# Attention and two MoE layers on one core: row minima over two PSUM banks at once, small steps moved between engines, a new order

## The chip, the core and the metric

One core of one Trainium2 chip. The metric is the device time of one execution in microseconds (us); the kernel before has a median of 949.46 us over 3 runs (949.44 to 949.78). The engines are called PE (TensorE; PEld is its weight load), DVE (VectorE), ACT (ScalarE), POOL (GpSimd) and SP (SyncE, which issues most DMAs). SBUF is the on-chip working memory; PSUM is the memory that PE writes, in 8 banks of 512 float32 per partition.

## The reference, cut to what matters

```python
B, H, S, D = (4, 8, 576, 64)
scores = q @ k.T / sqrt(D); causal mask; a = softmax(scores); local = a @ v
q_p = where(q > 0, q, exp(q) - 1) + 1                  # phi, which is elu + 1
mem_out = (q_p @ M_prev) / (q_p @ z_prev + 1e-6)
g = 1 / (1 + exp(-beta))                               # per head
x = g * mem_out + (1 - g) * local                      # to 2304 tokens x 512
h = x @ w_in;  y = (h * tanh(softplus(h))) @ w_out     # first layer, 512 -> 2048 -> 512
h = y @ w_in2; out = (h * sigmoid(h)) @ w_out2         # second layer, same sizes
```

All of it is float32. The kernel reaches float32 accuracy in the two layers by splitting each operand into a high and a low part in the rounded format fp32r and summing three products.

## The kernel before

**Attention.** There are 32 heads, taken in 16 pairs (`B * NP`), and `steps(p)` (from L494) makes the steps of pair p. The 576 rows of queries are five chunks: chunk 0 has 64 rows, chunks 1 to 4 have 128; chunk i needs `width(i)` = 64 + 128 i columns of scores, so 192, 320, 448 and 576. For each pair and each head j of it:

- loads: `ldkT`, `ldqT`, `ldnq`, `ldnv` on SP's queue (`load`, L455); those of keys and queries (`kT`, `qT`) feed PE, `nq` feeds phi, `nv` holds the values.
- scores: `s1` to `s3`, `s0` and, since one PSUM bank holds 512 columns, two halves `s40` and `s41` of 288 columns for chunk 4 (`score`, L590; `s0`, L631). They go to a ring "s" of four PSUM banks (`RINGS`), one matmul output in each.
- row minima (the scores are negated, so a minimum is what softmax wants): `r..` on DVE, one instruction `ttr` (L588) that adds the mask, writes the scores to SBUF (`sm`) and keeps the minimum of the row; a short second instruction then writes the minimum out (DVE_READ_ACCUMULATOR2). For chunk 4 there are two of them for each head, the second starting from the minimum of the first (`r4`, L599). 
- exponentials with row sums: `e..` on ACT (L615).
- phi: `phu` (ACT, L507, a relu), `phn` (POOL, L505, q minus relu), `phe` (ACT, L506, the exponential), `phf` (POOL, L508, the sum), `phz`, `phy` (POOL, L509, L512, times z), `phr` (DVE, L513, row sums), `phg` (POOL, L516, L517), `phd` (DVE, L519, reciprocal), `phq` (DVE, L520, times the softmax row sums), then `phm..` (POOL, L534, L539), which put phi beside the exponentials.
- PE transposes of these (`X1`, `X2`, `X3`, `W`, L486) into the PSUM ring "t", copies out of it to SBUF (`X1A` and so on; those listed in `ON_ACT` on ACT, L476, the others on DVE, L479), the products with the values (`Vhi`, `Vlo`, L692) and their scaling into `xT` (DVE, L696).

Ahead of it stand the gates: `exp` on ACT (L434), `sig` (five instructions on DVE, L437 to L441), `spread` (ACT, L446 to L452). Steps `phg`, `n00` and `zg` of pair 0 need them.

**The layers.** `Moe` runs 32 visits (layer, quarter of the 2048 hidden columns, block of tokens). Activations are split on ACT (L971) and DVE (L964). Weights come in 64 + 64 jobs: a load `ld` (L793), the absolute value `abs` (L804 on ACT for the first eight jobs, `first(job)`; L806 on DVE for the others), four bit steps `b0` to `b3` on DVE (L814, L816, L818, L821), and splits on ACT, POOL (first eight jobs; L847, L866, L869) and DVE. The first eight jobs run beside the attention. PE multiplies with the names psX, psW, psY (L1000 to L1002) and acc (L1068). The layers' PSUM and SBUF pools open (`open0`, `open1`) only when the last pairs' steps have given theirs back.

**What sets the order.** `Steps.plan` lists all steps with a planned duration, due times and rings, and issues for each engine, in order of planned time, the ready step with the smallest late time; `SHIFT` is a table of numbers added to the late times of groups of steps. The order on each engine is therefore fixed when the program is built; on the chip every engine takes its instructions in that order and waits at each for what it needs.

## Time and profile before

| | us |
|---|---|
| median of 3 runs | 949.46 |
| span of the profiled execution, first to last instruction | 949.0 |
| first product of the layers starts on PE | 181.64 |
| DVE's first row minimum starts | 13.98 |
| PE, DVE, ACT, POOL busy over the span | 921.2, 662.5, 498.9, 140.4 |

The span is read in four stretches: 14.5 us in which the first data and gates arrive, 167 us of attention, 763 us of the two layers, and 4.5 us in which the last block is drained and stored. A busy time is the union of an engine's instructions; two instructions in a row on one engine overlap in the records by some 0.07 us, so the step from one start to the next is that much shorter than the duration. A bracket behind a row is the time that the engine stood idle before it and what released it.

### The profile page before, as it was taken

To read this page: it belongs to the slowest core of one execution; us is meant where nothing else is said; L and a number is where in the kernel's file an instruction comes from. 1 tells how busy PE (TensorE), PEld (TensorE's weight loads), DVE (VectorE), ACT (ScalarE), POOL (GpSimd) and SP (SyncE) were. 2 spreads that over 40 slices of the span, in tenths; PEclk is the share of its full clock that TensorE was granted. 3 is DMA by queue.
4 is the path that set the end of the run, shared out by engine and by line. 5 is a ranking of instruction groups with operands and counts; after the bars stand their busy time and mean duration, and the time that the engine had idled before them with its cause. 6 is when DMAs were issued, how large, how long until landed. Compare 5 with 4: busy or idle time off the path is not lost.

```text
span 949.0 us, 17264 instructions
## 1 busy us (share of the span) xinstructions
PE 921.2 (97%) x6544; PEld 813.1 (86%) x6544; DVE 662.5 (70%) x1504; ACT 498.9 (53%) x1172; POOL 140.4 (15%) x223
## 2 busy tenths in 40 slices
PE   4989999999999999999999999999999999999998
PEld 2656666799999999999999999998999888989986
DVE  4899899988984558665957889766647765754333
ACT  5998899876654243433433647554533442433330
POOL 5688798300000000000000000000000000000000
PEclk9999999999999999999999999999999999999999
DMA  6546563666647403850375535704550374024412
GB/s 209 149 158 194 165 199 121 213 261 235 221 150 250 156 1 98 274 156 1 117 253 197 221 119 198 278 23 162 189 177 10 108 265 145 1 93 147 157 54 99
DMA packets 60034, 147.72 MB, mean 156 GB/s; under 512 B 7600, under 2 KB 25136, under 8 KB 59952
## 3 DMA queue, kind: packets, MB, share of 16 engines
q1 hardware_dynamic: 59808, 146.30, 45.4%
...
q10 hardware_dynamic: 144, 0.33, 0.1%
...
## 4 chain that ended last, share of the span: by engine, by line
PE 85%; DVE 4%; ACT 3%; POOL 3%; issue 2%; DMA 2%; SPq 0%; DVEq 0%; POOLq 0%
PE acc L1068 42%; PE psX L1000 7%; PE psX L1001 7%; PE psX L1002 7%; PE psY L1000 4%; PE psY L1001 4%; PE psY L1002 4%; DVE sm L588 2%; PE psW L1001 2%; PE psW L1002 2%; PE psW L1000 2%; PE ps_t L692 2%; PE ps_s L595 2%; PE ps_t L486 1%; ACT Ph L615 1%
## 5 line engine op out<-in xcount | busy, mean ns | idle before, releaser
L1068 PE MATMUL acc<-g,w 128*128 128x320 f32 (+1 forms) x1152 | 218.3, 337 | 0.0
L1068 PE MATMUL acc<-w,g 128*128 128x512 f32 x864 | 214.4, 394 | 0.0
L1068 PEld LDWEIGHTS acc<-g,w 128*128 128x128 f32 x1152 | 183.8, 188 | 13.1
L1068 PEld LDWEIGHTS acc<-w,g 128*128 128x128 f32 x864 | 157.8, 188 | 30.5
L1031 ACT COPY vt<-psX 128x256 f32<-128x256 f32 (+1 forms) x192 | 75.2, 398 | 154.8 <-PE psX L1002 146.0
L1089 DVE TENSOR_TENSOR xT<-acc,xT 128x512 f32<-128x512 f32 (+1 forms) x126 | 77.2, 613 | 93.8 <-PE acc L1068 92.9
L1041 DVE TENSOR_TENSOR g<-vt,g 128x512 fp32r<-128x512 f32 (+1 forms) x128 | 94.1, 754 | 35.4 <-ACT g L1040 34.7
L1029 DVE TENSOR_TENSOR vt<-psY,vt 128x256 f32<-128x256 f32 (+1 forms) x128 | 57.9, 456 | 87.1 <-ACT vt L1031 46.2
L1040 ACT CAST g<-vt 128x512 fp32r<-128x512 f32 (+1 forms) x128 | 83.4, 672 | 31.5 <-PE acc L1068 30.1
L1000 PE MATMUL psX<-x,w 128*128 128x320 f32 (+1 forms) x256 | 75.8, 296 | 0.0
L1001 PE MATMUL psX<-x,w 128*128 128x320 f32 (+1 forms) x256 | 75.7, 296 | 0.0
L1002 PE MATMUL psX<-x,w 128*128 128x320 f32 (+1 forms) x256 | 75.6, 295 | 0.0
L595 PE MATMUL ps_s<-kT,qT 64*128 64x288 f32 (+3 forms) x320 | 66.8, 480 | 6.3 <-DMA kT<-in_kT_dram 4.6
L1037 ACT ACTIVATE vt<-vt 128x640 f32<-128x640 f32 (+1 forms) x64 | 43.8, 685 | 51.8 <-DVE vt L1029 51.5
L588 DVE CUSTOM_DVE_ANT_0 sm<-ps_s,mask 128x288 f32<-128x288 f32 (+3 forms) x128 | 56.9, 472 | 5.4 <-PE ps_s L595 3.1
L1035 ACT ACTIVATE vt<-vt 128x256 f32<-128x256 f32 (+1 forms) x64 | 28.5, 445 | 59.7 <-DVE vt L1029 59.7
L1036 ACT ACTIVATE vt<-psX 128x256 f32<-128x256 f32 (+1 forms) x64 | 26.0, 407 | 50.2 <-PE psX L1002 50.1
L1029 DVE TENSOR_TENSOR vt<-psW,vt 128x256 f32<-128x256 f32 (+1 forms) x64 | 29.1, 455 | 31.7 <-PE psW L1002 31.2
L1000 PEld LDWEIGHTS psX<-x,w 128*128 128x128 f32 x256 | 48.2, 188 | 2.0 <-issue 0.2
L1001 PEld LDWEIGHTS psX<-x,w 128*128 128x128 f32 x256 | 48.3, 189 | 1.7
L875 ACT CAST w<-val 128x512 fp32r<-128x512 f32 (+1 forms) x64 | 34.8, 567 | 26.5 <-DVE val L866 13.1
L1002 PEld LDWEIGHTS psX<-x,w 128*128 128x128 f32 x256 | 48.3, 188 | 0.0
...
## 6 DMA issues: line engine op xcount, KB each, us to landing
...
```

The source lines that it names most:

```text
L588: nc.vector.tensor_tensor_reduce(out, ps, mask, -0.125, init, ALU.add, ALU.min, acc)
L595: nc.tensor.matmul(ps, lhsT=s["qT"][R[j], qcols(i)], rhs=s["kT"][R[j], k0 + cols.start:k0 + cols.stop], start=True, stop=True)
L1000: nc.tensor.matmul(o, lhsT=W(0, kc), rhs=X(0, kc), start=(n in (1, 2, 7) and kc == 0), stop=False, skip_group_check=True)
L1001: nc.tensor.matmul(o, lhsT=W(0, kc), rhs=X(1, kc), start=False, stop=False, skip_group_check=True)
L1002: nc.tensor.matmul(o, lhsT=W(1, kc), rhs=X(0, kc), start=False, stop=(kc == 1), skip_group_check=True)
L1029: nc.vector.tensor_tensor(o, self.bank[q, to], o, op=ALU.add)
L1031: f[f"s{n}"] = lambda n=n: nc.scalar.copy(val(*at[n]), self.bank[q, "X"])
L1037: f["m2"] = lambda: nc.scalar.activation(val(1), val(1), fn)
L1040: f[f"h{c}"] = lambda c=c: nc.scalar.copy(hi(c), val(c))
L1041: f[f"l{c}"] = lambda c=c: nc.vector.tensor_tensor(self.gt(q, c)[:, 1, :2 * tb], val(c), hi(c).bitcast(F32), op=ALU.subtract)
L1068: nc.tensor.matmul(y, lhsT=a, rhs=b, start=(c == 0 and k == 0), stop=(c == 1 and k == 5))
L1089: nc.vector.tensor_tensor(part, acc, part, op=ALU.add)
```

## The change

Six things are changed, and the order of all engines is planned anew.

- **Row minima.** The ring "s" holds two units of two banks in place of four banks. For chunk 4 the two halves of a head lie in one unit, and one `ttr` of 576 columns reads both banks; for chunks 1 to 3 the two heads lie in the two banks of a unit; `s0` lies beside `s1`. A unit comes free when all that it holds is read. `sm` has five buffers for four; several small tiles have three or four buffers for two.
- **Gates.** Of `sig` DVE keeps the reciprocal; the other four small instructions go to POOL.
- **phi.** `phu` is relu(-q), `phe` exp of its negative, so that `phe` follows `phu` directly on ACT; `phn` adds q and `phu` in place into `nq`, which `phf` now frees.
- **phq** goes from DVE to POOL.
- **X2B**, a copy of 384 columns for each pair, goes from ACT to DVE.
- **abs** of the first eight weight jobs goes from ACT to DVE. These jobs may be planned from 6 us on, one in 16 us (before 20 and 20).

The planner gets new durations (`ps2`, `act2`, weights, POOL's splits), a rule (`port`, `lock`) by which some DVE steps and POOL's steps don't overlap in the plan, dependences that put each pair's scores behind the chunk 4 scores of the pair before, and a new `SHIFT`.

```diff
+                    if e == "D" and k in self.lock:
+                        d += max(0.0, port["G"] - now)
+                        port["D"] = now + d
+                    if e == "G":
+                        d += max(0.0, port["D"] - now)
+                        port["G"] = now + d
...
-ON_ACT = ("WA", "X1A", "X2A", "X2B", "X3A")
+ON_ACT = ("WA", "X1A", "X2A", "X3A")
...
+    E("phe", "A", 0.58, ["phu"])
...
-    E("phe", "A", 0.58, ["phn"])
-    E("phf", "G", 1.37, ["phe", "phu"])
-    E("phz", "G", 1.25, ["phf"])
+    E("phf", "G", 1.37, ["phe", "phn"])
+    E("phz", "G", 1.25, ["phf", "phe"])
     E("phy", "G", 0.29, ["phf"])
     E("phr", "D", dve(576), ["phz", "phy"])
-    E("phg", "G", 0.4, ["phr"])
+    E("phg", "G", 0.45, ["phr"])
...
-            n = SA if i == 4 else width(i)
-            E(f"s4{x}" if i == 4 else f"s{i}", "P", mm(n, 4), qk)
+            E(f"s4{x}" if i == 4 else f"s{i}", "P", mm(SA if i == 4 else w, 4), qk)
         for j in range(2):
-            w = width(i)
+            E(f"r{i}{j}", "D", dve(w) + 0.01, ["s40", "s41"] if i == 4 else [f"s{i}"], 0.17)
+            E(f"e{i}{j}", "A", act(w, False, 2), [f"r{i}{j}"])
+            m.uses.append(("sm", f"r{i}{j}", [f"r{i}{j}"], [f"e{i}{j}"]))
             if i == 4:
-                for x in range(2):
-                    E(f"r4{j}{x}", "D", dve(SA) + 0.067 * x, [f"s4{x}"] + ([f"r4{j}0"] if x else []), 0.17)
-                    m.uses.append(("s", f"s4{x}{j}", [f"s4{x}"], [f"r4{j}{x}"]))
-                dep = [f"r4{j}1"]
-            else:
-                E(f"r{i}{j}", "D", dve(w), [f"s{i}"], 0.17)
-                m.uses.append(("s", f"s{i}{j}", [f"s{i}"], [f"r{i}{j}"]))
-                dep = [f"r{i}{j}"]
-            E(f"e{i}{j}", "A", act(w, False, 2), dep)
-            r = f"r4{j}0" if i == 4 else f"r{i}{j}"
-            m.uses.append(("sm", r, [r], [f"e{i}{j}"]))
+                m.uses.append(("s", f"s4{j}", ["s40", "s41"], [f"r4{j}"]))
+        if i in (2, 3):
+            m.uses.append(("s", f"s{i}", [f"s{i}"], [f"r{i}0", f"r{i}1"]))
         if i == 1:
-            m.group("s", ("s0", "P", 0.17, qk), [("r00", "D", dve(ST), ["s0"], 0.17)])
+            E("s0", "P", 0.17, qk)
+            E("r00", "D", dve(ST), ["s0"], 0.17)
+            m.uses.append(("s", "s1", ["s1", "s0"], ["r10", "r11", "r00"]))
...
-            E("phq", "D", 0.12, ["za", "phd"])
+            E("phq", "G", 0.22, ["za", "phd"])
...
-    RINGS = {"s": 4, "t": 4, "sm": 4}
+    RINGS = {"s": 2, "t": 4, "sm": 5}
...
-        "nq": ([P, 9, D], F32, ["ldnq"], ["phn", "phu"], 2),
+        "nq": ([P, 9, D], F32, ["ldnq"], ["phf"], 2),
...
-        "e": ([P, 9, D], F32, ["phn"], ["phmh", "phml", "phm0"], 2),
+        "e": ([P, 9, D], F32, ["phe"], ["phmh", "phml", "phm0"], 2),
...
-        "c": ([P, 9], F32, ["phr"], ["phmh", "phml", "phm0"], 2),
+        "c": ([P, 9], F32, ["phr"], ["phmh", "phml", "phm0"], 4),
...
-        "P0": ([P, 3, ST], F32, ["e00", "phm0"], ["X3"], 2),
+        "P0": ([P, 3, ST], F32, ["e00", "phm0"], ["X3"], 3),
...
-    TILES["R"] = ([P, S - ST], F32, ["Rl"], ["Vhic", "Vloc"], 2)
+    TILES["R"] = ([P, S - ST], F32, ["Rl"], ["Vhic", "Vloc"], 3)
...
+    def unit(self, p, i, j):
+        s = self.st[p]
+        k = f"S4{j}" if i == 4 else f"S{i}"
+        if k not in s:
+            s[k] = self.ps["s"].tile([P, 2, 512], F32, tag="s", name="ps_s")
+        return s[k]
...
+        def one():
+            nc.gpsimd.tensor_scalar(bt, bt, 1.0, None, op0=ALU.add)
...
         def sig():
-            nc.vector.tensor_scalar(bt, bt, 1.0, None, op0=ALU.add)
             nc.vector.reciprocal(self.g, bt)
-            nc.vector.tensor_scalar(self.g1, self.g, -1.0, 1.0, op0=ALU.mult, op1=ALU.add)
-            nc.vector.tensor_scalar(self.g1c, self.g1, 1e-20, None, op0=ALU.max)
-            nc.vector.tensor_tensor(self.btg, self.g1c, bt, op=ALU.mult)
...
+        def rest():
+            nc.gpsimd.tensor_scalar(self.g1, self.g, -1.0, 1.0, op0=ALU.mult, op1=ALU.add)
+            nc.gpsimd.tensor_scalar(self.g1c, self.g1, 1e-20, None, op0=ALU.max)
+            nc.gpsimd.tensor_tensor(self.btg, self.g1c, bt, op=ALU.mult)
...
-        f["phn"] = lambda: nc.gpsimd.tensor_tensor(self.get(p, "e"), s["nq"], s["u"], op=ALU.subtract)
-        f["phe"] = lambda: nc.scalar.activation(s["e"], s["e"], AF.Exp)
-        f["phu"] = lambda: nc.scalar.activation(self.get(p, "u"), s["nq"], AF.Relu)
-        f["phf"] = lambda: nc.gpsimd.tensor_tensor(s["e"], s["e"], s["u"], op=ALU.add)
+        f["phu"] = lambda: nc.scalar.activation(self.get(p, "u"), s["nq"], AF.Relu, scale=-1.0)
+        f["phe"] = lambda: nc.scalar.activation(self.get(p, "e"), s["u"], AF.Exp, scale=-1.0)
+        f["phn"] = lambda: nc.gpsimd.tensor_tensor(s["nq"], s["nq"], s["u"], op=ALU.add)
+        f["phf"] = lambda: nc.gpsimd.tensor_tensor(s["e"], s["e"], s["nq"], op=ALU.add)
         f["phz"] = lambda: nc.gpsimd.tensor_tensor(
             self.get(p, "u")[:, :8].rearrange("p (c j) d -> p c j d", j=2), s["e"][:, :8].rearrange("p (c j) d -> p c j d", j=2),
             self.bt[b]["z"][:, h0:h0 + 2, :].unsqueeze(1).to_broadcast([P, 4, 2, D]), op=ALU.mult)
-        f["phy"] = lambda: nc.gpsimd.tensor_tensor(s["u"][:, 8], s["e"][:, 8], self.bt[b]["y"][:, hp], op=ALU.mult)
+        f["phy"] = lambda: nc.gpsimd.tensor_tensor(self.get(p, "u")[:, 8], s["e"][:, 8], self.bt[b]["y"][:, hp], op=ALU.mult)
...
-        f["phq"] = lambda: nc.vector.tensor_tensor(s["c"][:, :8], s["c"][:, :8], s["z"][:, :8], op=ALU.mult)
+        f["phq"] = lambda: nc.gpsimd.tensor_tensor(s["c"][:, :8], s["c"][:, :8], s["z"][:, :8], op=ALU.mult)
...
             for j in range(2):
-                ps = s[f"S{i}{j}{x}"] = self.psum("s")[:, :cols.stop - cols.start]
+                ps = self.unit(p, i, j)[:, x if i == 4 else j, :cols.stop - cols.start]
...
                 nc.tensor.matmul(
                     ps, lhsT=s["qT"][R[j], qcols(i)], rhs=s["kT"][R[j], k0 + cols.start:k0 + cols.stop],
                     start=True, stop=True)
-        def r4(j, x):
-            t = smt(4, j) if x == 0 else s[f"sm4{j}"]
-            m = G("m4")
-            cs = slice(x * SA, (x + 1) * SA)
-            init = BIG if x == 0 else m[:, 2 + j:3 + j]
-            acc = m[:, 2 + j:3 + j] if x == 0 else m[:, j:j + 1]
-            ttr(t[:, cs], s[f"S4{j}{x}"], self.mcols(j, S)[:, cs], init, acc)
...
         def ri(i, j):
             w = width(i)
-            ttr(smt(i, j), s[f"S{i}{j}"], self.mcols(j, w), BIG, G(f"m{i}")[:, j:j + 1])
+            sm, mask = smt(i, j), self.mcols(j, w)
+            if i == 4:
+                sm, mask = (t.rearrange("p (x k) -> p x k", x=2) for t in (sm, mask))
+                ps = self.unit(p, i, j)[:, :, :SA]
+            else:
+                ps = self.unit(p, i, j)[:, j, :w]
+            ttr(sm, ps, mask, BIG, G(f"m{i}")[:, j:j + 1])
...
         for j in range(2):
-            for x in range(2):
-                f[f"r4{j}{x}"] = lambda j=j, x=x: r4(j, x)
-            for i in (3, 2, 1):
+            for i in (4, 3, 2, 1):
...
-            s["S00"] = self.psum("s")[:, :ST]
+            s["S00"] = self.unit(p, 1, 0)[:, 0, width(1):width(1) + ST]
             for j in range(2):
...
-        m.add(("gate", "sig"), "D", 1.0, [("gate", "exp")], sig, 26.0)
-        m.add(("gate", "spread"), "A", 1.0, [("gate", "sig")], spread, 28.0)
+        m.add(("gate", "one"), "G", 0.2, [("gate", "exp")], one, 25.5)
+        m.add(("gate", "sig"), "D", 0.12, [("gate", "one")], sig, 26.0)
+        m.add(("gate", "rest"), "G", 0.6, [("gate", "sig")], rest, 27.0)
+        m.add(("gate", "spread"), "A", 0.75, [("gate", "rest")], spread, 28.0)
...
-                deps = [(p, x) for x in deps] + ([("gate", "spread")] if p == 0 and n in self.GATED else [])
-                if p > 1 and n in ("s40", "s41"):
-                    deps += [(p - 2, x) for x in self.SC + ["s0"]]
+                deps = [(p, x) for x in deps] + ([("gate", "spread")] if n in self.GATED else [])
+                if p and n in ("s40", "s41"):
+                    deps += [(p - 1, "s40"), (p - 1, "s41")] + [(p - 2, x) for x in (self.SC + ["s0"] if p > 1 else [])]
+                if p and n in ("s3", "s2", "s1", "s0"):
+                    deps += [(p - 1, "s40"), (p - 1, "s41")]
...
-            if self.first(job):
-                nc.scalar.activation(c, self.raw[job][:, :, 1].bitcast(F32), AF.Abs)
-            else:
-                nc.vector.tensor_scalar(
-                    c.bitcast(U32), self.raw[job][:, :, 1].bitcast(U32), 0x7FFFFFFF, None, op0=ALU.bitwise_and)
+            nc.vector.tensor_scalar(
+                c.bitcast(U32), self.raw[job][:, :, 1].bitcast(U32), 0x7FFFFFFF, None, op0=ALU.bitwise_and)
...
-            for x, e, d, deps in (("ld", "S", 2.2, []), ("abs", "A", 0.53, ["ld"]) if first else ("abs", "D", 0.465, ["ld"]),
...
+            for x, e, d, deps in (("ld", "S", 2.2, []), ("abs", "D", 0.335, ["ld"]),
...
+                if e == "D":
+                    m.lock.add(J(x))
...
+                m.lock.update(K(x) for x in ["l" + x for x in XOPS] + ["T1", "T2", "T3", "T4"])
...
-    ('gate', 'exp'): -1546.35, ('gate', 'sig'): -1000.81, ('gate', 'spread'): -1110.7, ('a', 'ldkT'): -1506.04,
...
+    ('gate', 'exp'): -11714.19, ('gate', 'one'): -139.64, ('gate', 'sig'): -170.94, ('gate', 'rest'): -4059.43,
```

The rows below are from the order of instructions that the built programs hold: a bracket names the engines (PE_, Pool_, Activation_, DVE_) or DMA queues (DMAHW..) whose semaphore the instruction waits for; ISA is `ttr` and, on an `m_` alone, the writing out of the minimum.

DVE at the very start, before: `warm` is a set-up step, the five rows after it are the gates (`bt_102` holds exp(-beta)), and the last is the first row minimum, of pair 0's chunk 4.

```order
L409 MEMSET warm 128x1
L437 TENSOR_SCALAR bt_102<-bt_102 128x8 [waits Activation_49]
L438 RECIPROCAL g<-bt_102 128x8 [waits DVE_49]
L439 TENSOR_SCALAR g_104<-g 128x8 [waits DVE_49]
L440 TENSOR_SCALAR g1c<-g_104 128x8 [waits DVE_49]
L441 TENSOR_TENSOR btg<-g1c,bt_102 128x8 [waits DVE_49]
L588 ISA sm,m_157<-ps_s,mask 128x288 [waits PE_49,Pool_49]
```

DVE at the same place, now: 320, 448, 64 and 192 columns are pair 0's chunks 2, 3, 0 and 1 (one row of each stands here), 576 its chunk 4.

```order
L420 MEMSET warm 128x1
L603 ISA sm,m_144<-ps_s,mask 128x320 [waits PE_49,Pool_49]
...
L603 ISA sm,m_157<-ps_s,mask 128x448 [waits PE_49]
...
L603 ISA sm,m_171<-ps_s,smask 128x64 [waits PE_49,Pool_49]
...
L603 ISA sm,m_174<-ps_s,mask 128x192 [waits Activation_49]
...
L451 RECIPROCAL g<-bt_102 128x8 [waits Pool_49]
L603 ISA sm,m_199<-ps_s,mask 128x576 [waits PE_49,Activation_49]
```

The gates stood ahead of DVE's first row minimum; now the one that is left on DVE stands behind all of pair 0's minima but those of chunk 4, which come last of the pair.

PE at the same place, before: four matmuls of 288 columns (pair 0's chunk 4), then the small ones of chunk 0 for pairs 0 and 1.

```order
L595 MATMUL ps_s<-kT,qT 128x288 [waits DMAHW3_49,DMAHW0_49]
L595 MATMUL ps_s<-kT,qT 128x288 x3
L634 MATMUL ps_s<-kT,qT 64x64 [waits DVE_49]
L634 MATMUL ps_s<-kT,qT 64x64
L634 MATMUL ps_s<-kT,qT 64x64 [waits DMAHW1_49,DMAHW0_49,DVE_49]
```

PE now, up to the first row that needs pair 1's keys and queries (the second last):

```order
L610 MATMUL ps_s<-kT,qT 128x320 [waits DMAHW3_49,DMAHW0_49]
L610 MATMUL ps_s<-kT,qT 128x320
L610 MATMUL ps_s<-kT,qT 128x448 x2
L610 MATMUL ps_s<-kT,qT 128x192 [waits DVE_49]
L610 MATMUL ps_s<-kT,qT 128x192
L645 MATMUL ps_s<-kT,qT 64x64 x2
L610 MATMUL ps_s<-kT,qT 128x288 [waits DVE_49]
L610 MATMUL ps_s<-kT,qT 128x288 [waits DVE_49,PE_49]
L610 MATMUL ps_s<-kT,qT 128x288 x2
L610 MATMUL ps_s<-kT,qT 128x448 [waits DMAHW3_49,DMAHW0_49,DVE_49]
L610 MATMUL ps_s<-kT,qT 128x448
```

Chunk 4, which takes the whole ring, came first; now it comes fourth, and its first matmul waits for DVE to have read chunk 3.

DVE in the middle of the attention, now, from the last row minimum of one pair (chunk 2, 320 columns) to the first of the next (chunk 4, 576): `xT` rows scale finished products, `h_` and `W_` rows are copies out of PSUM, `val` rows are bit steps of a weight job.

```order
L603 ISA sm,m_1681<-ps_s,mask 128x320 [waits Activation_49]
L603 ISA m_1681 128x1
L707 TENSOR_TENSOR xT<-ps_t,R 128x256 [waits DMAHW7_49,DMAHW0_49]
L494 COPY h_1654<-ps_t 128x6x64
L707 TENSOR_TENSOR xT<-ps_t,R 128x256 [waits PE_49]
L826 TENSOR_SCALAR val<-val 128x512 [waits DVE_49]
L494 COPY h_1728<-ps_t 128x6x64 [waits PE_49]
L494 COPY W_1730<-ps_t 128x64
L828 TENSOR_SCALAR val<-val 128x512 [waits DVE_49]
L603 ISA sm,m_1759<-ps_s,mask 128x576 [waits PE_49,Activation_49]
```

DVE at a like place, before: the minima of chunk 4 in four pieces follow chunk 1's (192 columns) after three other rows.

```order
L588 ISA sm,m_1427<-ps_s,mask 128x192 [waits PE_49,Activation_49]
L588 ISA m_1427 128x1
L696 TENSOR_TENSOR xT<-ps_t,R 128x256 [waits PE_49]
L816 TENSOR_SCALAR val<-val 128x512 [waits DVE_49]
L479 COPY W_1398<-ps_t 128x2x4x64 [waits PE_49]
L588 ISA sm,m_1492<-ps_s,mask 128x288 [waits PE_49,Activation_49]
L588 ISA m_1492 128x1
L519 RECIPROCAL c<-c 128x9 [waits Pool_49]
```

Between the last minimum of one pair and the first of the next stood three other instructions; now there are seven.

## Rows read from the trace of the kernel before

**Rows 1.** Stretches: length, busy PE, PEld, DVE, ACT, POOL, then PE clock, DMA, GB/s.

```profile
0.00:14.50 14.50, 2.29 (x8) 1.27 (x8) 3.53 (x9) 3.96 (x10) 6.60 (x14) 1.00 0.76 259
14.50:181.60 167.10, 156.03 (x1812) 105.34 (x1812) 151.60 (x540) 153.61 (x468) 132.05 (x208) 0.98 0.52 162
181.60:944.50 762.90, 762.90 (x4727) 706.47 (x4724) 506.64 (x956) 341.34 (x695) 1.80 (x1) 1.00 0.44 153
```

**Rows 2.** Instructions in order of time, start to 21 us: PE, ACT, DVE.

```profile
4.65 2.29 PE L595 MATMUL ps_s<-kT,qT 64*128 64x288 f32 x8 [4.65 <-DMA kT<-in_kT_dram]
14.51 0.86 PE L634 MATMUL ps_s<-kT,qT 64*64 64x64 f32 x8 [7.57 <-DVE m L588]
...
6.15 0.68 ACT L507 ACTIVATE u<-nq 128x576 f32<-128x576 f32 x1 [3.92 <-DMA nq<-in_q_dram]
10.08 0.68 ACT L507 ACTIVATE u<-nq 128x576 f32<-128x576 f32 x1 [3.25 <-DMA nq<-in_q_dram]
10.66 0.19 ACT L434 ACTIVATE bt<-bt 128x8 f32<-128x8 f32 x1
...
10.89 1.37 DVE L437 TENSOR_SCALAR bt<-bt 128x8 f32<-128x8 f32 x1 [10.03 <-ACT bt L434]
13.98 0.46 DVE L588 CUSTOM_DVE_ANT_0 sm<-ps_s,mask 128x288 f32<-128x288 f32 x1
19.86 0.75 DVE L513 TENSOR_REDUCE c<-u 128x9 f32<-128x576 f32 x1
20.80 0.35 DVE L588 CUSTOM_DVE_ANT_0 sm<-ps_s,mask 128x192 f32<-128x192 f32 x1
```

**Rows 3.** Groups by line and shape, 0 to 182 us: busy, mean ns | idle before.

```profile
L588 DVE CUSTOM_DVE_ANT_0 sm<-ps_s,mask 128x448 f32<-128x448 f32 x32 | 19.1, 617 | 2.8 <-PE ps_s L595 2.2 <-ACT Ph L615 0.5
L588 DVE CUSTOM_DVE_ANT_0 sm<-ps_s,mask,m 128x288 f32<-128x288 f32 x32 | 15.7, 508 | 0.3 <-PE ps_s L595 0.3
L588 DVE CUSTOM_DVE_ANT_0 sm<-ps_s,mask 128x320 f32<-128x320 f32 x32 | 15.0, 481 | 0.8 <-PE ps_s L595 0.5 <-ACT Ph L615 0.3
L588 DVE CUSTOM_DVE_ANT_0 sm<-ps_s,mask 128x288 f32<-128x288 f32 x32 | 13.8, 444 | 1.5 <-ACT Pl L615 0.9 <-PE ps_s L595 0.3
L479 DVE COPY h<-ps_t 128x384 f32<-128x384 f32 x16 | 8.6, 540 | 0.7 <-PE ps_t L486 0.6
L520 DVE TENSOR_TENSOR c<-c,z 128x8 f32<-128x8 f32 x16 | 7.1, 444 | 0.0
L814 DVE TENSOR_SCALAR val<-val 128x512 f32<-128x512 f32 x8 | 6.0, 754 | 1.7 <-ACT val L804 1.7
L816 DVE TENSOR_SCALAR val<-val 128x512 uint32<-128x512 uint32 x7 | 4.3, 615 | 0.0
...
L517 POOL TENSOR_TENSOR c<-c,bt 128x9 f32<-128x9 f32 x16 | 3.3, 204 | 1.3
```

**Rows 4.** Instructions that touch two tiles: ns min/median/max, first and last start.

```profile
L520 DVE TENSOR_TENSOR c<-c,z x16: 101/298/1201, 24.3 to 174.8; 128x8 f32<-128x8 f32 x16
...
L806 DVE TENSOR_SCALAR val<-stg x56: 415/419/429, 188.1 to 822.9; 128x512 uint32<-128x512 uint32 x56
```

**Rows 5.** A weight job's step on DVE and the POOL instruction beside it, in time.

```profile
194.61 1.52 DVE L814 TENSOR_SCALAR val<-val 128x512 f32<-128x512 f32 x1
...
194.05 1.80 POOL L847 TENSOR_TENSOR w<-val,w 128x512 fp32r<-128x512 f32 x1 [15.69 <-ACT w L842]
```

**Rows 6.** Who waited for whom, 14 to 182 us on DVE, then to 182 on POOL.

```profile
DVE sm L588 <- PE ps_s L595: 3.4, 6, 1.3
DVE c L513 <- POOL u L512: 2.1, 4, 0.8
DVE val L814 <- ACT val L804: 1.7, 1, 1.7
...
POOL e L508 <- ACT e L506: 11.6, 7, 2.9
```

More of the change, by code (lines that the diff above doesn't have):

```diff
@@ L118, in plan @@
         mode = 0
+        port = {"D": 0.0, "G": 0.0}
         passed = {}
@@ L452, in spread @@
                 nc.scalar.copy(self.g1s[r, :], gv[r, j, :])
-        return exp, sig, spread
+        return exp, one, sig, rest, spread
     def load(self, p, nm, queue=None):
@@ L766, in ps2 @@
 def ps2(n):
-    return 0.126 + n / 960
+    return 0.07 + n / 960
 def sb1(n):
@@ L886, in register @@
             first = self.first(job)
-            slow = 0.05 if first else 0.0
-            for x, e, d, deps in (("ld", "S", 2.2, []), ("abs", "A", 0.53, ["ld"]) if first else ("abs", "D", 0.465, ["ld"]),
-                                  ("b0", "D", 0.465, ["abs"]), ("b1", "D", 0.465, ["b0"]), ("b2", "D", 0.735, ["b1"]),
-                                  ("b3", "D", 0.735, ["b2"])):
-                m.add(J(x), e, d + (slow if e == "D" else 0.0), [J(y) for y in deps], f[x], t,
-                      lag=1.6 if x == "ld" else 0.0, after=20.0 + 20.0 * n if first and x == "ld" else 0.0)
+            for x, e, d, deps in (("ld", "S", 2.2, []), ("abs", "D", 0.335, ["ld"]),
+                                  ("b0", "D", 0.335, ["abs"]), ("b1", "D", 0.335, ["b0"]), ("b2", "D", 0.6, ["b1"]),
+                                  ("b3", "D", 0.6, ["b2"])):
+                if e == "D":
+                    m.lock.add(J(x))
+                m.add(J(x), e, d, [J(y) for y in deps], f[x], t,
+                      lag=1.6 if x == "ld" else 0.0, after=6.0 + 16.0 * n if first and x == "ld" else 0.0)
             m.hold("W.raw", job, [J("ld")], [J("b3")], order=n)
```

21 lines of the change are left out of this document (12 added, 9 removed), and 198 rows, old and new, of the table SHIFT.

## The prediction

> **What bounds the kernel now.** I read the four stretches first [rows 1]. From 181.6 us to 944.5 us, the two layers, PE is busy 762.90 of 762.90 us: nothing outside PE's own columns sets that stretch, and the change leaves the layers' matmuls as they are. The last 4.5 us are a drain and a store. So the time is the moment S at which the layers' first product starts (181.6), plus 767.4 (762.9 + 4.5), plus the 0.46 by which the median of 949.46 stands above the profiled span of 949.0. Only S can move by much, and the question is what sets S.
>
> The second row says that no single engine does: in the 167.1 us of attention PE is busy 156.0, ACT 153.6, DVE 151.6 and POOL 132.1. Three engines are above 90%, and each has idle time of 11 to 16 us that the others cause. An edit that only moves work from one of them to another is worth little there. The first row is different: in the first 14.5 us PE does 2.3 us of work, ACT 4.0, DVE 3.5, none of which is a row minimum. So I read that stretch in order of time [rows 2]. Keys and queries are there at 4.65, PE makes four matmuls in 2.29 us and then stands for 7.57 us, waiting for DVE to free the ring. DVE stands for 10.03 us because its first instruction is a gate, which waits for ACT; ACT stands for 3.25 us because the second pair's `nq`, landing at 10.08, is in front of the gate's exponential in its queue. Then DVE works on gates until 13.98. All three big engines start some 8 us after they could.
>
> **The change, part by part.** First the start, by the order of the changed kernel. PE's first matmuls are now of 320 columns. Eight records of 288 took 2.29, a quarter of which is 0.57 for one matmul; two of 320 columns take 1.27, so DVE can begin at 4.65 + 1.27 + 0.2 = 6.1 (0.2 is my estimate of the hand-over). I walk on with the same PE rate and with durations of DVE [rows 3] less the 0.07 by which neighbours overlap. Chunk 2: 6.1 to 6.9. Chunk 3's two matmuls (448 columns, 1.78) end at 7.7, its minima at 8.8. Chunks 1 and 0 end on PE at 8.7, on DVE at 9.5. The gate's reciprocal comes then; its input needs ACT's exponential behind only one `nq` (6.15 + 0.68 + 0.19) and one POOL instruction behind pair 0's first phi step, some 8.5, so it waits for nothing. Chunk 4's matmuls get their first unit when chunk 3 is read (8.8 + 0.2) and end 2.29 later, at 11.4; the two wide minima (0.68 each, below) run 11.6 to 13.0, the row sum of phi (0.75 - 0.07) to 13.7. Before, DVE had all of this, and 0.3 us of later pairs' chunk 0, done at 20.80 + 0.27 = 21.1 (phi's row sum at 19.86, pair 0's last minimum at 20.80) [rows 2]. The lead is 21.1 - 0.3 - 13.7 = **7.1**; I take 7.0. It is a lead of PE and ACT too, since they follow these minima. Bounds: 7.9 (13.98 - 6.1), and 3.5 if pair 1's queries, which PE wants at 11.4, come late: that load is now behind two other loads on SP's queue, and `nq`, issued at a like place before, landed at 10.08.
>
> Then DVE's work up to the layers' first split, counted in the order.
> - Wide minima: 32 times 444 + 508 ns become 32 times one. 320 to 448 columns costs 136 ns more [rows 3], so 576 costs 753; the saving is 199 less one overlap of 70, 32 x 0.13 = **-4.1**. The trace shows no read across two banks: it may cost as much as the second start (then 0); I take the straight line, since each half alone lies on it.
> - `phq` leaves: 16 x (0.444 - 0.07) = **-6.0**. On POOL it is 16 x 0.204 = 3.3 (the like 128x9 step) [rows 3], and with the gates about 4 us, inside POOL's 35 us of idle; behind it on POOL wait the two `phm` steps and, for them, PE's transposes, so with that cover gone it costs these 3.3.
> - X2B arrives: 16 x (0.540 - 0.07) = **+7.5**; ACT loses 16 copies of its own.
> - abs arrives eight times. The nearest rows are the same operation on the same tile in this stretch, L814 and L816, means 0.754 and 0.615: 8 x 0.61 = **+4.9**. Alone it takes 0.42 [rows 4], which gives 2.8; beside POOL one such step took 1.52 [rows 5], which gives 11.6. ACT loses these eight too; with the copies, at DVE's prices, that makes it some 12 us lighter.
> - Planned ahead of the split are also one b0 and one b1 more and two copies of 512 columns fewer: nothing, to 0.1.
>
> DVE's sum is +2.3 (bounds -0.9 and +13, the latter with every abs behind a POOL instruction and no gain from the wide read).
>
> Third, waits [rows 6]. DVE's 1.7 for an abs on ACT goes, since DVE makes it. POOL's 11.6 for `phe` goes, since `phe` no longer waits for POOL, so DVE's 2.1 for POOL's `u` may halve: together **-2.7** (bounds 0 and -5, ACT being lighter). The 3.4 us that DVE waits for scores I leave. `nq` is now freed by `phf`, one POOL step later; its loads are issued a pair ahead, so that costs nothing, and if it does, it is a wait like the 3.25 of ACT [rows 2], with SP's row-sum transfers queued behind it.
>
> The layers' new order I cost at nothing: PE is covered there by work on all sides (DVE 507 and ACT 341 of 763) [rows 1].
>
> The sum: -7.0 + 2.3 - 2.7 = -7.4, so S is 174.2, the span 941.6, the median **942.1**.
>
> **Where the notes speak against it.** `phq` on DVE took 444 ns in the mean, though its shortest was 101 [rows 4], and POOL does the like step in 204 [rows 3]. The Trainium skill (GPSIMD Engine Reference, 4.1 Engine selection) says the opposite of the edit: elementwise work belongs on VectorE, GPSIMD being about twice as slow for two inputs. Both hold for the bare durations; by the rule alone the step would be worth 16 x 0.03 on DVE and the time would be 947.6. I go by the mean. The abs steps: one L814 ran 1.52 us while POOL's L847 ran beside it, and L806 after POOL's work is over never took more than 0.429 [rows 4, 5]. The Trainium skill (SBUF, Who interferes with whom) has a rule for this: a VectorE `tensor_scalar` in its two-port mode and a GpSimd instruction exclude each other, and the later one blocks until the first is done. The trace agrees; by the rule at its worst all eight wait, and the time would be 948.8.
>
> **The rivals.**
> - *The ring of two units stalls DVE* (slower). Chunk 4 needs both units, and PE can't start it before chunks 3 or 2 and 1 of the pair before are read; DVE has no minimum to take for four matmuls and two hand-overs, at the start's rate 2.3 + 0.4 = 2.7 us. Against it: the order puts seven other steps there, at 0.4 to 0.6 each some 3 us. For it: those steps wait themselves for PE, which stands in the same queue, and the longest wait of DVE for scores was already 1.3 [rows 6]. With 1.3 in each of 15 pairs the stall is 19.5, less the gain of 7.4: 961.6; with 10 us 952.1. It decides from 7.4 / 15 = 0.5 us a pair.
> - *The new order clears the port* (faster still). L814 and L816 lose 0.335 and 0.196 a time against their shortest, the four bit steps together some 7 us, and the planner now keeps them apart from POOL. If half of that and the abs' 2.1 go: 937.5.
> - *The start does not gain* (about the same). Pair 1's loads, moved behind pair 0's values on SP's queue, come some 3.5 us late, and idle stays: 942.1 + 3.5 + 2.7 = 948.3. The change then doesn't do what its start says.
> - *The layers' order opens gaps* (slower). Every step there has a new place. Against it: PE's 762.90 of 762.90. If PE waits 9.5 us in all for late splits or weights, the time is 951.6.
>
> **How the numbers follow.** Forecast 0.56 (938 to 946), port cleared 0.14, no gain at the start 0.10, ring stalls 0.15, gaps 0.05. A measurement of this kernel can tell about 0.2%, 1.9 us, from no change, so faster is below 947.6 and slower above 951.4. Faster: 0.56 + 0.14 and a third of the start case, 0.73; same: the rest of that case and the mild end of the ring's, 0.10; slower 0.17. The range from 936.0 to 949.5 holds the first three cases and leaves out the ring, the gaps and the far end of the cleared port.
>
> **What would show it.** Right: DVE's first row minimum near 6 us, phi's first row sum near 13, the first product near 174, PE full after it; `ttr` of 576 columns near 0.75; DVE's waits for scores not above some 4 us in all; abs between 0.42 and 0.8. Wrong: DVE's waits on PE for scores of 0.5 us and more in most pairs; a first row sum of phi after 17; a first product later than 178; PE idle in the layers.

## The result, and the profile after

The kernel after takes **940.93 us** (median of 4 runs, 940.20 to 941.86) where before takes 949.62 beside it. The ratio on record is 0.9902, 95% interval 0.9887 to 0.9917 (the two medians alone divide to 0.9908). The forecast was 942.1. The sum behind it agrees less well than the total, as the places where the time went show; each difference is taken between the two profiled executions, whose spans are 949.0 and 940.1:

| | before | after | change | forecast |
|---|---|---|---|---|
| phi's first row sum starts on DVE | 19.86 | 12.88 | -7.0 | -7.0 |
| layers' first split starts on DVE | 179.44 | 166.75 | -12.7 | -7.4 |
| from there to the layers' first product | 2.20 | 0.52 | -1.7 | 0 |
| from the first product to PE's last | 762.88 | 768.33 | +5.4 | 0 |
| from PE's last to the end of the span | 4.5 | 4.5 | 0 | 0 |

So the attention gained 5.3 us more than was worked out, and the way from it to the end gave 3.8 back.

The stretches of after, cut as in [rows 1] (length, busy PE, PEld, DVE, ACT, POOL, then PE clock, DMA, GB/s):

```profile
0.00:14.50 14.50, 8.02 (x28) 4.41 (x30) 5.24 (x21) 7.90 (x26) 8.61 (x20) 1.00 0.74 259
14.50:167.30 152.80, 144.40 (x1785) 98.74 (x1781) 145.60 (x464) 138.01 (x426) 134.12 (x223) 1.00 0.56 175
167.30:935.60 768.30, 766.32 (x4738) 707.87 (x4736) 500.22 (x959) 342.51 (x700) 1.29 (x1) 1.00 0.44 152
```

In the start PE now does 8.0 us of work and not 2.3. In the last row PE is no longer busy throughout: 1.98 us of 768.30 are idle, where before had none.

The start in order of time, PE, ACT and DVE, answers [rows 2]:

```profile
4.72 3.57 PE L610 MATMUL ps_s<-kT,qT 64*128 64x320 f32 x12 [4.72 <-DMA kT<-in_kT_dram]
13.58 2.93 PE L610 MATMUL ps_s<-kT,qT 64*128 64x448 f32 x8 [1.53 <-DMA qT<-in_qT_dram]
...
12.71 0.68 ACT L520 ACTIVATE u<-nq 128x576 f32<-128x576 f32 x1 [1.92 <-DMA nq<-in_q_dram]
...
6.32 0.49 DVE L603 CUSTOM_DVE_ANT_0 sm<-ps_s,mask 128x320 f32<-128x320 f32 x1 [5.47 <-PE ps_s L610]
9.56 0.20 DVE L451 RECIPROCAL g<-bt 128x8 f32<-128x8 f32 x1
11.35 0.76 DVE L603 CUSTOM_DVE_ANT_0 sm<-ps_s,mask 128x576 f32<-128x576 f32 x1 [1.59 <-PE ps_s L610]
12.88 0.75 DVE L528 TENSOR_REDUCE c<-u 128x9 f32<-128x576 f32 x1
15.59 0.62 DVE L603 CUSTOM_DVE_ANT_0 sm<-ps_s,mask 128x448 f32<-128x448 f32 x1 [1.96 <-PE ps_s L610]
```

The walk of the prediction stands here nearly to the tenth: first minimum 6.32 (6.1), the gate's reciprocal 9.56 without a wait (9.5), the first wide minimum 11.35 (11.6), phi's row sum 12.88 to 13.63 (ending 13.7). Then comes what was kept as a bound: pair 1's queries land at 13.5, PE stands 1.53 us for them and DVE 1.96.

Groups of the attention by line and shape (busy, mean ns | idle before), for [rows 3], and who waited for whom, for [rows 6]:

```profile
L603 DVE CUSTOM_DVE_ANT_0 sm<-ps_s,mask 128x576 f32<-128x576 f32 x32 | 23.3, 745 | 1.9 <-PE ps_s L610 1.9
L494 DVE COPY h<-ps_t 128x384 f32<-128x384 f32 x32 | 17.3, 540 | 0.2 <-PE ps_t L501 0.2
L818 DVE TENSOR_SCALAR val<-stg 128x512 uint32<-128x512 uint32 x8 | 6.8, 852 | 1.5 <-DMA stg<-in_moe_w_out_dram 1.5
...
L535 POOL TENSOR_TENSOR c<-c,z 128x8 f32<-128x8 f32 x16 | 3.7, 232 | 0.2
```

```profile
DVE sm L603 <- PE ps_s L610: 9.8, 5, 5.5
DVE sm L603 <- PE ps_s L645: 1.0, 4, 0.5
DVE c L528 <- POOL u L527: 0.5, 1, 0.5
...
POOL e L523 <- ACT e L521: 3.4, 5, 1.4
```

A minimum over two banks takes 745 ns (753 forecast), phq on POOL 232, an abs 852. Of DVE's 9.8 for scores 5.5 lie ahead of the first minimum, so 4.3 are left, with 1.0 more for those of chunk 0 (L645). POOL's wait for phe fell from 11.6 to 3.4. DVE's wait of 1.7 for an abs on ACT is gone, and in its place DVE waits 1.5 for a weight load (L818).

### The profile page after: what moved, and what is told of

Read it like the earlier page. It is cut to its first block, busy times and chain, and to the rows that moved or that the text cites. A ratio compares the mean times of both kernels' runs of the same rounds, so it can differ in the third digit from the quotient of the medians.

```text
span 940.1 us, 17127 instructions
## 1 busy us (share of the span) xinstructions
PE 918.7 (98%) x6544; PEld 811.0 (86%) x6544; DVE 651.8 (69%) x1444; ACT 488.4 (52%) x1150; POOL 144.0 (15%) x243
## 4 chain that ended last, share of the span: by engine, by line
PE 85%; DVE 8%; DMA 3%; ACT 2%; issue 1%; POOL 1%; SPq 0%; DVEq 0%; ACTq 0%
PE acc L1081 42%; PE psX L1013 7%; PE psX L1014 7%; PE psX L1015 7%; PE psY L1013 4%; PE psY L1015 4%; PE psY L1014 4%; DVE sm L603 3%; PE ps_t L703 2%; PE ps_s L610 2%; PE psW L1014 2%; PE psW L1013 2%; PE psW L1015 2%; PE ps_t L501 1%; DVE h L494 1%
## 5 line engine op out<-in xcount | busy, mean ns | idle before, releaser
L1081 PE MATMUL acc<-g,w 128*128 128x320 f32 (+1 forms) x1152 | 210.4, 337 | 0.0
L1081 PE MATMUL acc<-w,g 128*128 128x512 f32 x864 | 208.6, 394 | 0.0
L1054 DVE TENSOR_TENSOR g<-vt,g 128x640 fp32r<-128x640 f32 (+1 forms) x128 | 93.9, 754 | 47.1 <-ACT g L1053 46.6
L1053 ACT CAST g<-vt 128x640 fp32r<-128x640 f32 (+1 forms) x128 | 83.4, 673 | 70.7 <-PE acc L1081 69.8
L1042 DVE TENSOR_TENSOR vt<-psY,vt 128x320 f32<-128x320 f32 (+1 forms) x128 | 58.1, 455 | 76.9 <-PE psY L1015 45.9
L603 DVE CUSTOM_DVE_ANT_0 sm<-ps_s,mask 128x192 f32<-128x192 f32 (+3 forms) x128 | 66.7, 546 | 11.3 <-PE ps_s L610 9.8
L610 PE MATMUL ps_s<-kT,qT 64*128 64x288 f32 (+3 forms) x320 | 63.0, 482 | 10.0 <-DMA kT<-in_kT_dram 4.7
L1050 ACT ACTIVATE vt<-vt 128x512 f32<-128x512 f32 (+1 forms) x64 | 43.7, 685 | 33.3 <-DVE vt L1042 33.2
L610 PEld LDWEIGHTS ps_s<-kT,qT 64*128 64x128 f32 x320 | 30.1, 197 | 24.2 <-DVE m L603 10.9
L1049 ACT ACTIVATE vt<-psX 128x320 f32<-128x320 f32 (+1 forms) x64 | 26.2, 409 | 41.9 <-PE psX L1015 41.8
```

Of the source, the lines that this page charges most:

```text
L603: nc.vector.tensor_tensor_reduce(out, ps, mask, -0.125, init, ALU.add, ALU.min, acc)
L610: nc.tensor.matmul(ps, lhsT=s["qT"][R[j], qcols(i)], rhs=s["kT"][R[j], k0 + cols.start:k0 + cols.stop], start=True, stop=True)
L1042: nc.vector.tensor_tensor(o, self.bank[q, to], o, op=ALU.add)
L1050: f["m2"] = lambda: nc.scalar.activation(val(1), val(1), fn)
L1053: f[f"h{c}"] = lambda c=c: nc.scalar.copy(hi(c), val(c))
L1054: f[f"l{c}"] = lambda c=c: nc.vector.tensor_tensor(self.gt(q, c)[:, 1, :2 * tb], val(c), hi(c).bitcast(F32), op=ALU.subtract)
```

## The experiments

All start from the kernel after but for one that starts from before. Ratios are to the kernel before, which ran some 951.5 us on these chips, so 0.001 is 0.95 us. The kernel after itself ran once more among them (e5):

> The kernel after, unchanged, so that the three kernels beside it, and those that ran without it, have it on a chip of their own. Every theory: 0.990 of the kernel before, the first split near 166 us, the first product near 167.

It took 0.9888 (0.9872 to 0.9905), with the first split at 166.01 and the first product at 166.61. The others are held against this 0.9888, also those that ran on another chip. Each ratio is known to some 1.6 us either way, so I estimate that two of them differ clearly from some 2.2 us on.

Steps are moved by a few lines in `issue`, which take a step out of the planned order and put it behind another:

```diff
-        for k in self.plan():
+        seq = self.plan()
+        for k, behind in self.MOVES:
+            seq.remove(k)
+            seq.insert(seq.index(behind) + 1, k)
+        for k in seq:
```

**Is a microsecond at the start one at the end?** First the start is taken away (e1):

```diff
-            ttr(sm, ps, mask, BIG, G(f"m{i}")[:, j:j + 1])
+            for _ in range(20 if (p, i, j) == (0, 2, 1) else 1):
+                ttr(sm, ps, mask, BIG, G(f"m{i}")[:, j:j + 1])
```

> The kernel after, with its first row minimum issued twenty times (the same instruction, the same result). The trace of after has one such step at 0.40 us a time, so DVE, and with it PE and ACT, fall 19 x 0.40 = 7.6 us behind, which is the start that the change gained. If a microsecond at the start is a microsecond at the end, the time is 940.9 + 7.6 = 948.5. Rival: the attention has slack behind its start and another engine sets its end, so that most of the 7.6 is made up: 941 to 943.

It took 0.9982 (0.9971 to 0.9993), 8.9 us more than after. The repeats were dearer than 0.40: DVE in order of time, first repeats, then phi's first row sum:

```profile
6.39 0.49 DVE L603 CUSTOM_DVE_ANT_0 sm<-ps_s,mask 128x320 f32<-128x320 f32 x1 [5.54 <-PE ps_s L610]
6.81 0.08 DVE L603 DVE_READ_ACCUMULATOR2_ANT m<- 128x1 f32 x1
6.93 0.49 DVE L603 CUSTOM_DVE_ANT_0 sm<-ps_s,mask 128x320 f32<-128x320 f32 x1
```

Each starts 0.53 us behind the last, and phi's row sum starts at 23.09, 10.2 late. The first split was 8.4 late (175.18), PE's end 9.1. So most of a microsecond at the start, some 0.8 to 0.9, is one at the end; the rival falls. (PE, which stood for 9.76 us until 17.49, had a granted clock of 0.50 from 12 to 22 us, the lower of its two levels, 1.2 of 2.4 GHz; it is not told apart what that added to the end.)

Next the gate's part of the start alone, in the kernel before (e4):

```diff
+    MOVES = [(('gate', 'exp'), (0, 'phu')), (('gate', 'sig'), (0, 'r411')), (('gate', 'spread'), (0, 'e40'))]
```

> The kernel before, with three steps moved and nothing else: the gate's exponential ahead of pair 1's first phi step on ACT, the gate's five small steps on DVE behind the four minima of pair 0's chunk 4, its spread on ACT behind chunk 4's exponentials. The first row minimum then comes near 7.2 us instead of 13.98, and the gate's steps, 0.9 to 2.9 us, still stand on DVE; the lead is 4 to 6 us and the time, if the start carries through, 949.6 - 5 = 944.6 (943.6 to 945.6). Rival: the start is not what sets the end, the ring of four or the loads take it back: 948 to 950.

It took 0.9976 (0.9960 to 0.9992), a gain of 2.3 us, under half of the 5 that were expected. The first minimum came at 7.24 as expected, but phi's row sum only at 17.18, 2.7 earlier than in before, where the first minimum was 6.7 earlier. PE in order of time shows why:

```profile
7.76 0.48 PE L640 MATMUL ps_s<-kT,qT 64*64 64x64 f32 x4 [0.65 <-DVE m L594]
11.67 0.48 PE L640 MATMUL ps_s<-kT,qT 64*64 64x64 f32 x4 [3.42 <-DMA kT<-in_kT_dram]
```

In the order of before, pair 1's chunk 0 stands on PE ahead of pair 0's chunk 3, and PE waits 3.42 us for pair 1's keys. What did arrive at 17.18 went through to the end: the first split is 3.6 earlier, the span too, and the layers take 762.87 as before. So moving the gate gives under half of the start's 7. The rest came with the new order, which takes all of pair 0's chunks first; no run has that order without the changes to gates, phi and the ring, but with the four parts below undone (e8) phi's first row sum still starts at 12.74.

Last, the wait that is left (e2):

```diff
+    MOVES = [((0, 'ldnv'), (1, 'ldnq')), ((2, 'ldkT'), (0, 'ldnv')), ((1, 'ldqT'), (1, 'ldkT'))]
```

> The kernel after, with pair 1's queries and its token-major queries moved ahead of pair 0's values and pair 2's keys on SP's queue. In the trace of after PE stands for 1.53 us until 13.58 for pair 1's queries and DVE for 1.96 us until 15.59. If the start carries through, these are gained: 939.0 to 939.4. Rival: the values or pair 2's loads are late in their place, or the idle time comes back within some pairs: 940.9.

It took 0.9877 (0.9856 to 0.9897): 1 us less than after, which the interval doesn't tell from nothing. PE's wait for queries is gone and part of it is back as another:

```profile
11.38 2.73 PE L616 MATMUL ps_s<-kT,qT 64*128 64x448 f32 x8 [0.52 <-DVE m L609]
15.08 1.65 PE L507 MATMUL ps_t<-ident,Ph 64*128 64x64 f32 x26 [0.86 <-ACT Ph L634]
```

The first split came at 164.52; three executions with after's own order there had it at 165.28, 166.01 and 166.75, and another one with these moves (e11, below), whose DVE, ACT and POOL take the same instructions in the same order up to there, at 167.61. So whether any of the 1 us is real stays open.

**What is each part worth?** Four kernels with after's order and one of its parts undone in place. First the wide minima (e6):

```diff
-            if i == 4:
-                sm, mask = (t.rearrange("p (x k) -> p x k", x=2) for t in (sm, mask))
-                ps = self.unit(p, i, j)[:, :, :SA]
+            if i == 4:
+                m = G("m4")
+                for x in range(2):
+                    cs = slice(x * SA, (x + 1) * SA)
+                    ttr(sm[:, cs], self.unit(p, i, j)[:, x, :SA], mask[:, cs],
+                        m[:, 2 + j:3 + j] if x else BIG, m[:, j:j + 1] if x else m[:, 2 + j:3 + j])
+                return
```

> The kernel after in its order, but each of the widest minima in two instructions of 288 columns again. In the traces the two halves and their accumulator reads held DVE for 27.2 us in before and the wide ones for 21.6 in after, so DVE gets 5.6 us more. If DVE's own work sets the end of the attention, the time is after's + 5.6. Rival: DVE stands 10 us for others after its first minimum, and the work goes into these holes: after's + 0 to 2.

It took 0.9935 (0.9918 to 0.9951): the wide minima are worth **4.5 us** here. The rival, that holes take the work, falls.

Then `phq` (e7):

```diff
-        f["phq"] = lambda: nc.gpsimd.tensor_tensor(s["c"][:, :8], s["c"][:, :8], s["z"][:, :8], op=ALU.mult)
+        f["phq"] = lambda: nc.vector.tensor_tensor(s["c"][:, :8], s["c"][:, :8], s["z"][:, :8], op=ALU.mult)
```

> The kernel after in its order, but with the gate step phq on DVE again. It held DVE for 16 x 0.374 = 6.0 us in before, of which 5.5 was over its shortest. If the mean counts, the time is after's + 6.0. Rival, by the bare durations of 0.101 on DVE and 0.204 on POOL: after's + 0.5 or less, since the new order may keep the step apart from POOL's work.

It took 0.9954 (0.9938 to 0.9971): phq on POOL is worth **6.3 us**. On DVE, in this order too, its mean is far over its shortest of 106 ns:

```profile
L535 DVE TENSOR_TENSOR c<-c,z 128x8 f32<-128x8 f32 x16 | 6.3, 391 | 0.0
```

What makes it so long stands beside it on POOL. One of the long ones, and what POOL did then, both until 133.5:

```profile
132.23 1.29 DVE L535 TENSOR_TENSOR c<-c,z 128x8 f32<-128x8 f32 x1
132.09 1.41 POOL L522 TENSOR_TENSOR nq<-nq,u 128x576 f32<-128x576 f32 x1
```

Four of the 16 took 702 to 1367 ns, and each ended 23 to 26 ns behind the end of a POOL instruction that had started before it. In the kernel before it was nine of 16, with 276 to 1201 ns, ending 22 to 25 ns behind POOL's; the other seven took 101 to 157.

The copy X2B (e9):

```diff
-            return self.hi if n + a in ON_ACT else self.vec
+            return self.hi if n + a in ON_ACT + ("X2B",) else self.vec
```

> The kernel after in its order, but with the copy X2B on ACT again: DVE has 7.4 us less, ACT some 16 x 0.4 = 6.4 more, to which it has 16 us of idle time in the attention. If DVE's work sets the end, 0.989 of before falls to 0.982 (after's - 7). Rival: ACT is as full as DVE once it has it, and gives half back: after's - 2 to - 4, the value that two halves, phq and all four together leave for X2B and abs, + 7.5 - 4.6 - 6.4 = - 3.5. A second rival, that the copy pays for itself on DVE: after's + 1 to + 3.

It took 0.9887 (0.9869 to 0.9905): where the copy runs makes **no difference** that the interval shows, some 2 us either way. The 7 us of the first value are out; the near ends of the two rivals are not.

The first weights' abs (e10):

```diff
-            nc.vector.tensor_scalar(
-                c.bitcast(U32), self.raw[job][:, :, 1].bitcast(U32), 0x7FFFFFFF, None, op0=ALU.bitwise_and)
+            if self.first(job):
+                nc.scalar.activation(c, self.raw[job][:, :, 1].bitcast(F32), AF.Abs)
+            else:
+                nc.vector.tensor_scalar(
+                    c.bitcast(U32), self.raw[job][:, :, 1].bitcast(U32), 0x7FFFFFFF, None, op0=ALU.bitwise_and)
```

> The kernel after in its order, but with the first weights' abs on ACT again: DVE has 6.4 us less (8 x 0.80), ACT 8 x 0.6 = 4.8 more. If DVE's work sets the end: after's - 6. Rival: the three or four steps that follow an abs on DVE then wait for ACT, as one did in before for 1.7 us: after's - 1 to + 1.

It took 0.9899 (0.9884 to 0.9915), 1.0 us more than after, within the intervals: DVE's 6.4 us for the abs cost nothing that can be told.

**Why do X2B's 7.4 and the abs' 6.4 us on DVE cost nothing?** All four undone (e8), and then only the first two, the halves and phq (e12):

> The kernel after in its order, with all four parts undone: two halves for the widest minima, phq on DVE, the copy X2B and the first weights' abs on ACT. On DVE this is + 5.6 + 6.0 - 7.4 - 6.4 = -2.2 us, on ACT some + 11. What is left of the change is its order, the start with it. If DVE's sum sets the end: after's - 2. Rival: with 11 us more ACT becomes the bound, or the order is made for these places and does not suit others: after's + 5 to + 11, and the parts carry that much of the gain of 8.7.

> The kernel after in its order, with two parts undone, the two halves and phq on DVE, while X2B and abs stay on DVE. DVE then has 5.6 + 6.0 = 11.6 us more than after. Alone the two cost 4.4 and 6.3 us (0.9935 and 0.9954 of before, against 0.9888 for after), all four together 7.2. If DVE and ACT bound the attention together, DVE is now the only one, its work counts fully, and the two cost 10.7 to 11.6: 1.000 to 1.001 of before; X2B and abs on ACT, worth nothing in the kernel after, are then worth 3.5 to 4.4 here. Rival: the costs saturate because the order does not suit, whatever the engine: 7 us, 0.996 of before.

All four undone took 0.9964 (0.9950 to 0.9979), 7.2 us more than after, although DVE has less to do. With only the first two undone it was **1.0019** (1.0007 to 1.0032), 12.4 more than after: all of the gain is lost, and X2B and abs on ACT, worth nothing that can be told in after, are worth 5.2 us in that company. The theory of two bounds had 10.7 to 11.6 and 3.5 to 4.4, somewhat less than both; the rival of 7 us falls. The rows from first minimum to first split, of after, of all four undone, of X2B on ACT and of two undone (columns as above):

```profile
6.32:166.75 160.43, 150.27 (x1791) 101.40 (x1789) 150.23 (x483) 143.80 (x448) 140.29 (x231) 1.00 0.58 184
```

```profile
6.35:173.03 166.68, 152.22 (x1793) 100.61 (x1791) 149.20 (x539) 153.67 (x472) 136.41 (x215) 0.98 0.55 177
```

```profile
6.30:165.54 159.24, 150.96 (x1790) 100.49 (x1788) 145.13 (x467) 147.71 (x464) 140.87 (x231) 1.00 0.58 185
```

```profile
6.37:175.44 169.07, 154.34 (x1795) 101.99 (x1793) 160.21 (x564) 146.19 (x448) 136.99 (x215) 1.00 0.55 174
```

DVE and ACT are the third and fourth numbers behind the length. After: DVE 150, ACT 144. With all four undone ACT is the fuller with 154 and the stretch 6 us longer. With two undone DVE has 160 and the stretch is 169. With X2B on ACT they are level at 145 and 148 and nothing is gained against 150 and 144. So the length goes with the fuller engine where the two stand apart (10 us more on DVE made it 8.6 longer), and near balance a move between them changes little. Two things stay open. The profiled execution with two undone was one of the quickest of its twelve and that of after the slowest of its four, which accounts for most of the difference between the 8.6 us of these rows and the 12.4 of the ratios. And PE, the first number behind the length, is at 150 to 154 in all four, in after as full as DVE; no run tells whether PE holds the end there too.

**Where do the layers give back?** ACT in order of time in the kernel after, at the end of the first layer: its table loads, with the activations around them (L1048 to L1050):

```profile
532.80 0.42 ACT L1048 ACTIVATE vt<-vt 128x256 f32<-128x256 f32 x1 [0.97 <-DVE vt L1042]
535.39 1.28 ACT L1048 ACT_TABLE_LOAD   x1
536.68 0.47 ACT L1048 ACTIVATE vt<-vt 128x320 f32<-128x320 f32 x1
538.21 1.28 ACT L1049 ACT_TABLE_LOAD   x1
539.50 0.38 ACT L1049 ACTIVATE vt<-psX 128x256 f32<-128x256 f32 x1
553.86 1.28 ACT L1048 ACT_TABLE_LOAD   x1
```

The first layer's function is Mish, the second's Silu. The new order puts one Silu (at 536.68) between the last steps of Mish, so the table changes three times; before, it changed once, at 560. PE then stands (PE in order of time, same kernel):

```profile
542.10 0.41 PE L1015 MATMUL psY<-x1T,w 128*128 128x320 f32 x1 [1.01 <-DVE w L878]
```

The Trainium skill (ScalarE activation tables: per-element evaluation and per-set limits, What a function is on this engine) says that two functions of different sets are one load of 1283 ns apart; the rows agree, 1.28 each. The experiment moves that one Silu (e3):

```diff
+    MOVES = [(('Q', (16, 0), 'm11'), ('Q', (15, 1), 'm2'))]
```

> The kernel after, with one step moved: the first Silu of the second layer goes behind the last Mish of the first. The trace of after has three loads of ACT's function table between 535 and 554 us, 1.28 each, where before had one, and PE stands 1.2 us at 541 and 0.3 at 556. If the table loads make these gaps, both go, and the time is 940.9 - 1.5 = 939.4. Rival: the gap is the weights' second part, which DVE makes late for other reasons; then PE still stands there and the time is 940.9.

It took 0.9867 (0.9845 to 0.9889), 2 us below after; the intervals overlap, but the layers show it plainly: from first product to PE's end 766.30 us, where the ten profiled executions with after's own layers took 768.30 to 769.05. PE's waits from 165 us on, in after:

```profile
PE psY L1015 <- DVE w L878: 1.0, 1, 1.0
PE ps_t L501 <- DVE xT L707: 0.7, 1, 0.7
PE ps_t L580 <- DVE xT L707: 0.5, 1, 0.5
PE psX L1013 <- ACT vt L1044: 0.5, 1, 0.5
PE ps_t L703 <- ACT h L491: 0.4, 1, 0.4
```

and with the Silu moved:

```profile
PE psX L1019 <- ACT vt L1050: 0.5, 1, 0.5
PE ps_t L709 <- ACT h L497: 0.4, 1, 0.4
```

The wait for weights is gone with the two loads; the two with xT lie in the last of the attention, before the stretch that the second list covers after its shift of 1.5 us.

Last, all moves together, and one more for the 0.5 that is left on `vt` (e11):

```diff
+    MOVES = [((0, 'ldnv'), (1, 'ldnq')), ((2, 'ldkT'), (0, 'ldnv')), ((1, 'ldqT'), (1, 'ldkT')),
+             (('Q', (16, 0), 'm11'), ('Q', (15, 1), 'm2')), (('Q', (0, 0), 'm11'), ('Q', (0, 1), 's1'))]
```

> The kernel after with the moves of the earlier queries and of the one table change, and one more: the first Mish of the first layer behind the next copy on ACT, so that the table load at 174 us does not hold that copy, for which PE stands 0.46 us. The gains add up if they lie in different places: 0 to 2 + 2 + 0.5 below after, 0.985 to 0.988 of before, 937 to 938.5. Rival: the layers take back what the start gains, as they did with 3 to 4 us of the 12.7: no faster than with one table change alone, 0.9867.

It took 0.9867 (0.9846 to 0.9887), no faster than the one table change, so the rival holds. The new move missed: the wait on `vt` became longer, and the layers took 766.86.

```profile
PE psX L1019 <- ACT vt L1050: 1.0, 1, 1.0
```

So of these versions the change with its one Silu moved is the one to keep, some 1.3% below before; the earlier queries add nothing that can be told.

## Why the prediction was right, and where its working was not

**The start, -7.0: right.** Phi's row sum came 6.98 earlier, each step where the walk had it, and e1 shows that a microsecond there is worth 0.8 to 0.9. Of the bounds, the one at 3.5 named the right transfer (pair 1's queries), which cost some 1.5 to 2 us at most.

**Wide minima, -4.1, and phq, -6.0: right.** 745 ns against 753, and 4.5 and 6.3 us by taking each back. The step on the mean of 444 and not on the shortest of 101 was the right one. The Trainium skill (GPSIMD Engine Reference, 4.1 Engine selection) puts elementwise steps on VectorE; the run that follows it is slower by those 6.3. For so short a step beside a busy POOL the wait for it decides and not the bare duration, as the rows under e7 show.

**X2B, +7.5, and abs, +4.9: the step that failed.** DVE did get these (16 copies more at 540 ns; the abs 852 in the mean, between the bounds of 0.42 and 1.52), but the time did not. The sum took every microsecond of DVE's as one of the time. Its own first part said that PE, ACT and DVE were all above 90% and that work moved between them is worth little, and then credited ACT's 12 us of relief with only 2.7 in waits. Measured from the kernel after, moving them to ACT gains nothing: X2B 0.1 less and abs 1.0 more, each to some 2 us. From the kernel with halves and phq undone it gains 5.2, not the sum's 7.5 + 4.9. For the four parts the prediction had +2.3 - 2.7 = -0.4; e8 gives -7.2. DVE's work from first minimum to first split is 150 us in both kernels, where +2.3 was forecast; its idle time there fell from 15.5 to 10.2 us, where -2.7 was forecast. For before, the row like those under e12 names the engine that was relieved:

```profile
13.98:179.44 165.46, 153.87 (x1790) 103.98 (x1792) 149.96 (x539) 152.47 (x469) 132.05 (x208) 0.98 0.52 163
```

In before ACT was the fuller of the two with 152.5; after, it has 143.8, and the stretch is 5.0 us shorter at the same work on DVE. That this relief is what the waits term priced too low is argued from these rows: no run gives ACT its work back without taking as much from DVE.

**The layers' order at nothing: failed too.** PE 762.90 of 762.90 showed that the old order had no gap, not that a new one would have none. First product to PE's end grew by 5.4. Of it 2.0 come from the two more table loads, by e3 (PE's wait of 1.0, one of 0.1 and slowed steps beside them). 1.2 is attention work, products with the values, of which 3.3 us now run behind the first product and 2.1 did before; that is no loss, since S itself came 1.7 nearer to the split. 0.85 are the two gaps that e3 leaves. The last 1.4 or so are matmuls a little further apart, and were not followed. The traces hold three table loads in before and five in after. The alternation of Mish and Silu that calls for them stands in the planned order of ACT, so they could have been counted.

**Around the span, 0.46: mis-sized.** The four runs of after are each 1.8 us longer than their span; the 0.46 set before's median against the span of another execution.

So 5.3 us too little for the attention, 3.8 too much faith in the way behind it and 1.3 for the frame nearly cancelled: 0.2 us against the profiled execution of 941.86, 1.2 against the median. That the total came so near is luck; the start, the wide minima and phq were not.

**The signs and a bound.** First minimum, phi's first row sum and the 745 ns came as named. The first product came at 167.3 and not near 174, and PE stood for 1.98 us in the layers, which the prediction had named as a sign of being wrong. The abs (0.85) and DVE's waits for scores behind its first minimum (5.3 us with chunk 0) lie above their 0.8 and 4. The lower bound of -0.9 for DVE's sum does not follow from the bounds of its terms, which give +0.2; nothing else was worked out from it.

**The rivals.** The ring of two units did not stall DVE: 4.0 of the 4.3 us for scores lie ahead of 15.6 us, and behind that DVE waits 0.3 and, for chunk 0, 1.0 us in all, not 0.5 in each pair. The port was not cleared: an abs, 0.41 alone, took 0.85 in the mean, and a job's four bit steps together took 3.03 us in the mean, against 3.11 before. The start did gain. The layers' order did open gaps, in a smaller size than the 9.5 named.
